# Moving eleven DMA calls of a written-out schedule to later places

## The chip, the cores and the metric

The kernel runs on one core of one Trainium2 chip. The metric is device time in microseconds (us) of one launch. A core has a TensorE (PE, with its weight loads written PEld), a VectorE (DVE), a ScalarE (ACT), a GpSimd (POOL) and a SyncE (SP), and 16 DMA engines that its queues share. All data DMAs of this kernel are issued by SyncE.

## The reference

Two attention blocks, A and B, each on an input x of 2048 tokens by 640 channels, with 32 heads of 20. Their outputs lie side by side in the result.

```python
# A: attention over a sliding window of 256 tokens
qkv = x @ wqkv                                  # 640 x 1920
scores = einsum("bhqd,bhkd->bhqk", q, k) * Dh ** -0.5
mask = (i - j >= 0) & (i - j < 256)
o = einsum("bhqk,bhkd->bhqd", softmax(where(mask, scores, -1e9)), v);  a = o @ wo

# B: linear attention, not causal
phi = lambda t: where(t > 0, t + 1, exp(t)) + 1e-6
kv = einsum("bhsd,bhse->bhde", phi(k), v);  z = phi(k).sum over s
o = (phi(q) @ kv) / (phi(q) @ z + 1e-6);        b = o @ wo
out = concatenate([a, b], axis=-1)
```

## The kernel before

The 2048 tokens are four superblocks of 512 (s = 0 to 3). Block A's attention is cut into 76 score tiles (16 for s = 0, 20 for each other; `tiles_of`, line 39). One tile is a set of small score matmuls into one PSUM tile (L773), one exponential over it on ACT (L793), masks on POOL (L814), and, two tiles later, the products with the values (L841). These tiles follow one another in program order (the loop at line 1103).

Between tiles PE is filled with everything else: the projections q, k and v of A (`a_rows`, `a_v`), B's keys (`b_keys`), the sums of B's keys with its tokens (`b_sums`, L556), B's queries (`b_q`) and the output products. That filler work is a list `plan` of pairs (t, work), where t is in units of tiles. `at(t0, t1, gen, n)` spreads the n banks (PSUM tiles) of one generator evenly over t0 to t1; `do(t0, t1, fns)` does the same with plain calls, which here mostly issue DMAs. `fill_of` (line 1077) sorts all by t and runs through them; after each tile, `take` draws as many columns of matmul work from it as the tile's credit allows. A plain call yields no columns: it is made when the sorted list comes to it. So t sets the order of the work and only roughly its time.

All these DMAs go to SyncE's instruction stream (`nc.sync`) in the order in which the calls are made. SyncE takes them in order; when one has to wait (for its source to be written, or for its buffer to be free), all behind it wait too. The names that matter here:

- `load_part(n, s, tb)` (L958): transposes 128 tokens of x of block n, superblock s, from DRAM into xA or xB, 160 KB. `parts` makes four of them. xA and xB have two buffers each.
- `load_tok(s)` (L548): loads 512 tokens of B's x, not transposed, 640 KB, into `tok` (two buffers); `b_sums(half)` reads them for two superblocks at a time.
- `keep_x(s)` (L947) writes xB of superblock s to DRAM scratch, 640 KB; `again_x(s)` (L951) reads it back for `b_q`.
- `late_load("B", 2)` and `late_load("B", 0)` (L166): B's value and query weights, 800 KB each into wB.
- `moves` (L385, L394): A's q and k rows that need other partitions go through DRAM scratch. The four writes are posted with `soon(write, 3)`: they are made when the third PSUM bank after the last one of q or k is begun. The four reads are calls of the plan (`reads_of`); each first makes all posts that are still open.
- `turn` (L882): transposes A's normalised output within SBUF, also posted with `soon`.

Of the kernel before, what the change touches and what calls it, by code (L numbers as in the profile page):

```python
# [102 lines left out]
def kernel(  # L103
# [228 lines left out]
    for c in range(KT):  # L332
        m = EXTRA * c
        while m < EXTRA * (c + 1):
            n = min(EXTRA * (c + 1) - m, DH - m % DH)
# [209 lines left out]
    def load_tok(s):  # L545
        x_tok[s] = rp.tile([P, TPS, D], BF16, name="tok")
        src = xsrc["B"][s * SB : (s + 1) * SB, :].rearrange("(t p) d -> p t d", p=P)
        nc.sync.dma_start(out=x_tok[s], in_=src)  # L548
# [397 lines left out]
    def keep_x(s):  # L946
        nc.sync.dma_start(out=x_scr[s], in_=xB[s].rearrange("p k n -> p (k n)"))  # L947

    def again_x(s):
        xB[NS + s] = xp.tile([P, KT, SB], BF16, name="xB")  # L950
        nc.sync.dma_start(out=xB[NS + s].rearrange("p k n -> p (k n)"), in_=x_scr[s])  # L951
# [36 lines left out]
    def late_load(n, w):  # L988

        if w in (0, 2):  # L990
            load_w(n, B_wqkv, w, nc.sync)
        elif n == "A":

            wj = w.rearrange("(g j d) n -> g d j n", j=4, d=DH)
            for g in range(NG):
                lo, hi = g * DH, min((g + 1) * DH, P)
                if lo < P:
                    nc.sync.dma_start(out=wo_sb[n][lo:hi, 0:4, :], in_=wj[g, 0 : hi - lo])
            for j in range(4):
                for g in range(NG):  # L1000
                    lo, hi = max(g * DH, P), (g + 1) * DH
                    if hi > P:
                        nc.sync.dma_start(
                            out=wo_sb[n][32 * j + lo - P : 32 * j + hi - P, 4, :],
                            in_=wj[g, lo - g * DH : DH, j],
                        )
        else:
            g = GH * DH
            whole = w[0 : KT * g, :].rearrange("(c p) n -> p c n", p=g)
            nc.sync.dma_start(out=wo_sb[n][0:g, 0:KT, :], in_=whole)  # L1010
            nc.sync.dma_start(out=wo_sb[n][0 : D - KT * g, KT, :], in_=w[KT * g : D, :])
# [9 lines left out]
    def at(t0, t1, gen, n):  # L1021
        for i in range(n):
            plan.append((t0 + (i + 0.5) / n * (t1 - t0), gen, i == n - 1))

    def do(t0, t1, fns):
        fns = list(fns)
        for i, fn in enumerate(fns):
            plan.append((t0 + (i + 0.5) / len(fns) * (t1 - t0), None, fn))

    def parts(t0, t1, n, s):  # L1030
        do(t0, t1, [lambda tb=tb: load_part(n, s, tb) for tb in range(TPS)])
# [19 lines left out]
        at(t0, t1, b_keys(s), KT)  # L1051
    for half, t0, t1 in ((0, 16.4, 21.5), (1, 33.6, 39.2)):
        at(t0, t1, b_sums(half), KT + 2)
    for s, t in ((0, 6), (1, 11), (2, 23), (3, 24)):
        do(t, t, [lambda s=s: load_tok(s)])
    at(40.4, 42, b_kv(), 2)
    do(42.8, 44.8, [lambda c=c: kv_ready(c) for c in range(3)])
# [6 lines left out]
    for n, s, t0, t1 in (("A", 0, 44.5, 48.5), ("A", 1, 49.2, 54.2), ("B", 0, 55.2, 59.4),  # L1064
                         ("B", 1, 60.2, 64), ("A", 2, 64.4, 68.2), ("B", 2, 69, 73),
                         ("B", 3, 73, 76)):
        at(t0, t1, (a_out if n == "A" else b_out)(s), KT)
    for n, s, t0, t1 in (("B", 1, 5, 9), ("A", 2, 6, 12), ("B", 2, 14, 18), ("A", 3, 16, 24),
                         ("B", 3, 17, 22)):
        parts(t0, t1, n, s)  # L1070
    for s, t0, t1 in ((0, 2, 33.5), (1, 12, 38.5), (2, 20, 45.5), (3, 26, 51.2)):
        do(t0, t0, [lambda s=s: keep_x(s)])
        do(t1, t1, [lambda s=s: again_x(s)])
    for t, n, w in ((13, "B", 2), (20, "B", 0), (40.6, "A", A_wo), (42, "B", B_wo)):
        do(t, t, [lambda n=n, w=w: late_load(n, w)])

    def fill_of(events):
# [87 lines left out]
```

## Time and profile before

| what | value |
|---|---|
| median of three runs | 261.54 us (260.58 to 262.65) |
| the profiled execution | 260.71 us, span 259.0 us |
| TensorE (PE) busy | 245.9 us, 95% of the span |
| ACT busy | 199.9 us, 77% |
| DVE busy | 177.5 us, 69% |
| POOL busy | 171.1 us, 66% |
| data moved by DMA | 35.67 MB, 64.7% of the 16 DMA engines |
| mean granted TensorE clock | 1.000 |

Times in the rows of the profile count from the start of the span. A group's row has the line, the engine, the operation, its output and inputs, the count, and the time; a row of the waits has who waited, for whom, the total, the times and the longest. SPq is SyncE's own instruction queue, where a DMA's row is its issue, not its transfer. "issue" as releaser means that the engine waited for nothing that the profile shows. The rows that carry the argument stand in the prediction.

### The profile page before, as it was taken

What the parts mean: (1) busy time and instruction counts of PE and PEld (TensorE: products, weight loads), DVE (VectorE), ACT (ScalarE), POOL (GpSimd) and SP (SyncE); (2) the same over time, 40 slices, a digit from 0 to 9 for tenths busy, and PEclk for the clock granted to TensorE, in tenths of its full rate; (3) what the DMA queues carried; (4) which work ended last, traced back from release to release, by engine and by line L of the source; (5) the groups of instructions that cost most, each with busy time, mean ns of one, the idle gap of its engine ahead of it and who ended that gap; (6) DMA issues with size and microseconds to landing.
All of it is one profiled execution on the core that took longest, in us unless ns stands there. A gap on an engine that the chain in (4) does not pass through costs nothing.

```text
span 259.0 us, 10625 instructions
## 1 busy us (share of the span) xinstructions
PE 245.9 (95%) x4658; PEld 144.0 (56%) x4705; DVE 177.5 (69%) x308; ACT 199.9 (77%) x260; POOL 171.1 (66%) x211
## 2 busy tenths in 40 slices
PE   7899999999999599999999999999999999999995
PEld 7544446556556455545566655555556564565573
DVE  0445797687745156768656598599899879969562
ACT  3466879898876488887676888888979999988642
POOL 7115787778774845759475796949768595977700
PEclk9999999999999999999999999999999999999999
DMA  6995587889669791501454396534767699672735
GB/s 211 291 260 162 108 215 112 192 256 156 79 92 263 74 285 54 168 5 20 105 142 115 54 181 63 137 65 67 189 101 151 137 123 177 112 174 58 237 35 189
DMA packets 65012, 36.35 MB, mean 140 GB/s; under 512 B 48197, under 2 KB 63941, under 8 KB 64965
## 3 DMA queue, kind: packets, MB, share of 16 engines
q1 hardware_dynamic: 64965, 35.67, 64.7%
q8 instruction: 37, 0.61, 1.0%
q14 instruction: 10, 0.08, 0.1%
HBM read 14.42 MB, written 9.83 MB: 94 GB/s over the span
## 4 chain that ended last, share of the span: by engine, by line
PE 90%; DMA 4%; issue 3%; ACT 1%; SPq 1%; DVE 0%
PE dense L287 50%; PE S_ps L773 11%; PE dense L556 9%; PE dense L841 9%; PE dense L422 8%; DMA phi<-in_A_x_dram 2%; DMA xA<-tok 2%; PE dense L663 1%; PE dense L706 1%; PE dense L635 1%; ACT p L793 0%; SPq L968 0%; PE dense L188 0%; DVE wB L274 0%; SPq L182 0%
## 5 line engine op out<-in xcount | busy, mean ns | idle before, releaser
L793 ACT ACTIVATE p<-S_ps 128x2048 bf16<-128x2048 f32 x76 | 142.3, 1872 | 33.8 <-PE S_ps L773 32.7
L814 POOL TENSOR_SCALAR_AFFINE_SELECT p<-p 128x512 bf16<-128x512 bf16 (+1 forms) x152 | 122.7, 830 | 66.1 <-ACT p L793 63.7
L287 PE MATMUL dense<-xA,wqk 128*128 128x512 bf16 x183 | 47.3, 380 | 1.1 <-issue 0.6
L814 POOL TENSOR_SCALAR_AFFINE_SELECT plow<-p 128x1024 bf16<-128x1024 bf16 x32 | 40.0, 1250 | 0.0
L773 PE MATMUL S_ps<-qpad,kpad 20*128 20x64 bf16 (+3 forms) x1664 | 34.7, 211 | 0.4
L773 PEld LDWEIGHTS <-kpad 20*128 20x128 bf16 (+1 forms) x1664 | 20.1, 97 | 26.8 <-issue 25.5
L422 PE MATMUL dense<-wA,xA 128*128 128x320 bf16 x160 | 27.9, 300 | 3.6 <-issue 2.6
L854 DVE STREAM_TRANSPOSE T<-dense 128x512 f32<-128x512 f32 x32 | 22.8, 711 | 11.3 <-PE dense L841 11.3
L287 PEld LDWEIGHTS <-wqk 128*128 128x128 bf16 x200 | 18.5, 98 | 20.6 <-issue 1.3
L301 DVE TENSOR_SCALAR e<-e 128x512 bf16<-128x512 bf16 x40 | 22.1, 553 | 10.8 <-ACT e L297 10.0
L304 DVE SCALAR_TENSOR_TENSOR phi<-dense,e 128x512 bf16<-128x512 f32 x40 | 27.7, 691 | 1.5
L841 PE MATMUL dense<-p,vA 128*32 128x64 bf16 (+2 forms) x1152 | 26.2, 223 | 0.0
L287 PE MATMUL dense<-wB,xB 128*128 128x128 bf16 (+1 forms) x156 | 25.4, 298 | 0.8 <-issue 0.6
L297 ACT ACTIVATE e<-dense 128x512 bf16<-128x512 f32 x40 | 23.4, 594 | 3.0 <-PE dense L287 2.6
L287 PE MATMUL dense<-wo,oT 128*128 128x128 bf16 (+2 forms) x154 | 24.3, 296 | 1.1 <-issue 0.6
L287 PE MATMUL dense<-xB,wB 128*128 128x512 bf16 x90 | 24.2, 380 | 0.6 <-issue 0.3
L556 PE MATMUL dense<-phi,tok 128*128 128x128 bf16 (+1 forms) x154 | 24.3, 297 | 0.5 <-issue 0.3
L287 PE MATMUL dense<-wB,xA 128*128 128x512 bf16 (+1 forms) x156 | 23.4, 298 | 0.8 <-DMA xA<-tok 0.3
L841 PEld LDWEIGHTS <-vA 128*32 128x32 bf16 x1664 | 21.5, 97 | 2.7 <-issue 0.7
L422 PEld LDWEIGHTS <-xA 128*128 128x128 bf16 x160 | 14.4, 97 | 12.5 <-issue 4.8
L871 DVE TENSOR_TENSOR N<-T,recA 128x320 bf16<-128x320 f32 (+1 forms) x28 | 19.2, 685 | 2.9 <-DMA oT<-N 2.0
L272 ACT ACTIVATE osb<-dense 128x512 bf16<-128x512 f32 (+1 forms) x25 | 13.9, 571 | 6.7 <-PE dense L287 6.7
(68 smaller groups left out, 242.7 us busy)
## 6 DMA issues: line engine op xcount, KB each, us to landing
out_dram<-osb SPq DMA_DIRECT2D x7, 640.0 KB
x_scr<-xB SPq DMA_DIRECT2D x4, 640.0 KB
tok<-in_B_x_dram SPq DMA_DIRECT2D x4, 640.0 KB
xB<-x_scr SPq DMA_DIRECT2D x4, 640.0 KB
wB<-in_B_wqkv_dram SPq DMA_DIRECT2D x3, 800.0 KB
q_scr<-qpad SPq DMA_DIRECT2D x16, 60.0 KB
k_scr<-kpad SPq DMA_DIRECT2D x16, 60.0 KB
qpad<-q_scr SPq DMA_DIRECT2D x16, 60.0 KB
```

The lines of the kernel that those rows point to most:

```text
L287: nc.tensor.matmul(dst, lhsT=lhs(kt), rhs=rhs(kt), start=(kt == 0), stop=(kt == KT - 1))
L297: nc.scalar.activation(out=view(e), in_=src, func=ACT.Exp)
L301: nc.vector.tensor_scalar(out=e[:], in0=e[:], scalar1=1e-6, scalar2=1.0 + 1e-6, op0=ALU.add, op1=ALU.min)
L304: nc.vector.scalar_tensor_tensor(out=dst, in0=src, scalar=0.0, in1=view(e), op0=ALU.max, op1=ALU.add)
L422: nc.tensor.matmul(ps[:, 0 : hh * DH], lhsT=xt[:, kt, tb * P : (tb + 1) * P], rhs=w_sb["A"][:, kt, i * hh * DH : (i + 1) * hh * DH], start ...
L556: nc.tensor.matmul(out, lhsT=lhs(x, pk)[:, tb, :], rhs=rhs(pk, tb), start=(i == 0), stop=(i == len(blocks) - 1),)
L773: nc.tensor.matmul(columns(S_ps[0:keys], j, col, n, step), lhsT=kt[32 * j : 32 * j + DH, g, ko : ko + keys], rhs=q_pad[s][32 * j : 32 * j ...
L793: nc.scalar.activation(out=p.rearrange("p a j q -> p j a q"), in_=S_ps.rearrange("p j (a q) -> p j a q", a=2), func=ACT.Exp, scale=scale,)
L814: nc.gpsimd.affine_select(out=dst, in_=src, pattern=[[0, 4], [0, n // HALF], [sgn, HALF]], compare_op=ALU.is_ge, fill=0.0, base=base, chan ...
L841: nc.tensor.matmul(O_ps[32 * j : 32 * (j + 1), q0 : q0 + n], lhsT=v_flat[kb // TPS % 3][:, at + j * HV : at + j * HV + 32], rhs=of(p, j, c ...
L854: nc.vector.transpose(out=T.rearrange("p b e -> p (b e)"), in_=O_ps[:])
L871: nc.vector.tensor_tensor(out=dst[:, :, at : at + b - a], in0=T[:, :, a - lo : b - lo], in1=r[:].to_broadcast([P, SB // 32, b - a]), op=AL ...
```

## The change

Five lines of the plan are edited. `load_tok(2)` and `load_tok(3)` go from t = 23 and 24 to 24.2 and 28.2; B's fourth x (s = 3) from 17 to 22 to 19 to 25; A's fourth x from 16 to 24 to 25.5 to 33.5; `keep_x(2)` and `keep_x(3)` from 20 and 26 to 26.2 and 30.2; B's query weights from 20 to 32.2. No work is added or left out.

```diff
-    for s, t in ((0, 6), (1, 11), (2, 23), (3, 24)):
+    for s, t in ((0, 6), (1, 11), (2, 24.2), (3, 28.2)):
         do(t, t, [lambda s=s: load_tok(s)])
...
-    for n, s, t0, t1 in (("B", 1, 5, 9), ("A", 2, 6, 12), ("B", 2, 14, 18), ("A", 3, 16, 24),
-                         ("B", 3, 17, 22)):
+    for n, s, t0, t1 in (("B", 1, 5, 9), ("A", 2, 6, 12), ("B", 2, 14, 18), ("B", 3, 19, 25),
+                         ("A", 3, 25.5, 33.5)):
         parts(t0, t1, n, s)
-    for s, t0, t1 in ((0, 2, 33.5), (1, 12, 38.5), (2, 20, 45.5), (3, 26, 51.2)):
+    for s, t0, t1 in ((0, 2, 33.5), (1, 12, 38.5), (2, 26.2, 45.5), (3, 30.2, 51.2)):
         do(t0, t0, [lambda s=s: keep_x(s)])
         do(t1, t1, [lambda s=s: again_x(s)])
-    for t, n, w in ((13, "B", 2), (20, "B", 0), (40.6, "A", A_wo), (42, "B", B_wo)):
+    for t, n, w in ((13, "B", 2), (32.2, "B", 0), (40.6, "A", A_wo), (42, "B", B_wo)):
         do(t, t, [lambda n=n, w=w: late_load(n, w)])
```

## The prediction

> **What bounds the kernel now.** I read the page from the top: busy times, then the chain that ended last.
>
> ```profile
> PE 245.9 (95%) x4658; PEld 144.0 (56%) x4705; DVE 177.5 (69%) x308; ACT 199.9 (77%) x260; POOL 171.1 (66%) x211
> ...
> q8 instruction: 37, 0.61, 1.0%
> ...
> PE 90%; DMA 4%; issue 3%; ACT 1%; SPq 1%; DVE 0%
> ```
>
> TensorE is the bound: 95% of the span, 90% of the last chain. An edit that moves only DMAs can win only where PE stands still, and lose only where it makes PE stand. So the next view is PE's own waits from 14 us on, when the start-up is over, and the timeline row that ends the longest.
>
> ```profile
> PE dense L422 <- issue: 2.6, 1, 2.6
> PE dense L287 <- issue: 2.5, 16, 0.2
> PE dense L287 <- DMA xA<-tok: 0.3, 1, 0.3
> ```
>
> ```profile
> 87.52 0.58 PE L422 MATMUL dense<-wA,xA 128*128 128x320 bf16 x3 [2.64 <-issue]
> ```
>
> PE never waits for a late input of superblock 2. Apart from gaps of at most 0.2 us there is one hole, 2.64 us from 84.88 to 87.52, in the middle of one accumulation (L422), with nothing the profile can name as releaser. The page's row q8 suggests what it is: 37 packets with 0.61 MB, 16.5 KB each, and 4658 + 4705 PE instructions over 37 packets are 253 each. So PE's program comes by DMA in blocks of about 254 instructions. I asked the queue view, stretch by stretch, where such packets begin. In order: 85.0 to 85.2, 97.5 to 97.6, 110.1 to 110.2, 114.7 to 114.8, 129.05 to 129.15 us.
>
> ```profile
> q8 instruction: 1, 0.02, 29.1%
> ...
> q8 instruction: 1, 0.02, 60.3%
> ...
> q8 instruction: 1, 0.02, 59.2%
> ...
> q8 instruction: 1, 0.02, 83.2%
> ...
> q8 instruction: 1, 0.02, 70.7%
> ```
>
> (The share is of 16 DMA engines in that stretch: 0.291 x 0.2 x 16 = 0.93 us, and 0.96, 0.95, 1.33, 1.13 for the others.) The packet that begins at 85.1 lands at 86.0, and PE moves on 1.5 us later. I read the hole as PE out of instructions because this block was fetched late.
>
> Why late? These are SyncE's issues before and after, and what the DMA engines did.
>
> ```profile
> 78.09 0.53 SPq L947 DMA_DIRECT2D x_scr<-xB  x1
> 78.67 0.42 SPq L166 DMA_DIRECT2D wB<-in_B_wqkv_dram  x1
> 79.13 1.92 SPq L958 DMA_TRANSPOSE xB<-in_B_x_dram  x1
> 81.09 1.27 SPq L958 DMA_TRANSPOSE xA<-in_A_x_dram  x1
> 82.41 2.26 SPq L958 DMA_TRANSPOSE xB<-in_B_x_dram  x1
> 89.43 0.38 SPq L548 DMA_DIRECT2D tok<-in_B_x_dram  x1
> 89.86 1.25 SPq L958 DMA_TRANSPOSE xA<-in_A_x_dram  x1
> 91.20 0.52 SPq L548 DMA_DIRECT2D tok<-in_B_x_dram  x1
> 91.83 0.44 SPq L947 DMA_DIRECT2D x_scr<-xB  x1
> ```
>
> ```profile
> 79.20:81.50 2.30, 2.30 (x58) 1.49 (x57) 1.90 (x4) 1.36 (x2) 0.95 (x2) 1.00 0.97 266
> 81.50:84.10 2.60, 2.60 (x96) 2.31 (x89) 1.65 (x4) 1.92 (x2) 0.87 (x2) 1.00 1.05 331
> 84.10:88.00 3.90, 1.26 (x46) 0.89 (x46) 0.00 (x0) 2.56 (x4) 3.83 (x5) 1.00 1.18 118
> 90.30:98.20 7.90, 7.69 (x132) 4.21 (x135) 4.07 (x9) 6.93 (x8) 2.91 (x5) 1.00 0.87 267
> 102.80:107.60 4.80, 4.75 (x44) 2.60 (x42) 2.50 (x4) 4.34 (x5) 4.66 (x6) 1.00 0.56 110
> 107.60:110.00 2.40, 2.35 (x79) 1.46 (x79) 2.32 (x5) 2.15 (x3) 1.24 (x2) 1.00 0.67 259
> ```
>
> The last two columns are DMA share and GB/s. The x_scr write runs from 79.2 to about 81.5 (2.3 us, 1.1 us after its issue), wB to 84.1 (2.6, some of it beside transposes), the three 160 KB transposes to 88.0 (1.3 each). The first of these three is done near 85.2, and the instruction packet begins at 85.1, before the two issued after 81.1. That looks like **one line**: a packet waits for everything queued before it. Three more cases agree. The packet at 97.5 comes as the four transfers issued from 89.43 to 92.3 end (98.2); that at 110.1 as the transfer issued at 106.43 ends (110.0); and the packets at 114.7 and 129.1 met a short line or none. By the Trainium skill, "DMA: Bandwidth & Descriptors", section "Queues, rings and completion order", each DMA engine goes round the queue rows packet by packet, by which an instruction packet would wait for one data packet and not for microseconds; the packets at 85.1, 97.5 and 110.1 speak against that. "Runtime: NRT & Kernel Launch", section "Instruction fetch mechanics", has 16 KiB refills "mostly hidden"; the size agrees with row q8, the hiding fails once here.
>
> **The change part by part.** No operation is added or removed. PE, DVE, ACT and POOL keep their order, since these events yield no columns to the filler. Moved are eleven calls, all SyncE DMAs: B's and A's fourth x (four transposes each), `load_tok(2)` and `(3)`, `keep_x(2)` and `(3)`, and B's q weights. SyncE issues in order and runs ahead until an instruction has to wait, so what counts is not the t of a call but which wait it comes to stand behind. These are the waits there are, and the issues after them.
>
> ```profile
> SPq L548 <- PE dense L556: 4.9, 1, 4.9
> ...
> SPq L385 <- DVE kpad L274: 13.9, 1, 13.9
> SPq L385 <- DVE qpad L274: 6.2, 1, 6.2
> ```
>
> ```profile
> 102.02 1.63 SPq L385 DMA_DIRECT2D q_scr<-qpad  x4
> 104.29 2.09 SPq L394 DMA_DIRECT2D qpad<-q_scr  x4
> 106.43 0.35 SPq L951 DMA_DIRECT2D xB<-x_scr  x1
> 120.75 1.62 SPq L385 DMA_DIRECT2D k_scr<-kpad  x4
> ...
> 128.26 0.59 SPq L951 DMA_DIRECT2D xB<-x_scr  x1
> ```
>
> *Step 1, ahead of `load_tok(2)`.* Only three of B's transposes stay there. Without A's and with keep_x(2) and wB gone, SyncE is through by about 77 us and waits for `tok` (its buffer is freed by L556 at 89.4, the 4.9 us of the first row; 2.6 us earlier if the hole goes). The DMA engines are idle at 81 us. The block that began at 85.1 is then fetched without a line. I take it that a block is asked for when PE enters the last one it holds, 254 instructions before it runs dry. The rows above count 96 + 89 from 81.5 to 84.1 and some 80 of the 46 + 46 up to the hole, so that is at about 81.5. To be there by 84.88 the packet must begin by 84.88 - 1.5 - 0.95 = 82.4: 0.9 us in hand. **-2.64 us**.
>
> *Step 2, `tok`(2), B's last transpose, keep_x(2)* go out from 86.8 us: 2.0 + 1.3 + 2.3 us of DMA against 7.9 us before, with an instruction packet near 95. No loss.
>
> *Step 3, behind the q_scr write.* The third bank after q's last is b_keys(2)'s last, t 26.48, just ahead of A's first transpose at 26.5; so the q_scr write, which waits for qpad until 102.02, now has **seven** moved calls behind it, between the q reads and again_x(0): in order A 0, a q read, tok(3), a q read, A 1, two q reads, keep_x(3), A 2, wB, A 3, again_x(0). Nothing in this list waits again; the next wait is the k_scr write at 120.75. So they aren't spread up to t 32.5, they go out in one run. SyncE's time by the rows above: 1.63 + 4 x 1.3 + 4 x 0.4 + 0.45 + 0.55 + 0.45 is 9.9 us, with up to 1 us more for a transpose behind a full line (the 2.26 at 82.41); again_x(0) goes out at 111.9 to 112.9 in before's time. DMA time: q writes and reads 2.7 (0.56 x 4.8), four transposes 5.2, tok 2.0 (640 KB at the 331 GB/s of the second row; the 7.9 us at 90.3 less 1.3 and 2.3 leaves 2.1 each for its two), keep_x 2.3, wB 2.4, again_x 1.9 (1.6 of it in the last row): 16.5 us. It begins 1.1 us after 102.02 and loses 0.2 to gaps, as I estimate: the line is empty at about **119.8**.
>
> *Step 4, which instruction block meets it.* PE passed 632 matmuls and 640 weight loads between 87.5 and 119.8:
>
> ```profile
> 87.50:119.80 32.30, 31.66 (x632) 18.02 (x640) 21.62 (x39) 26.22 (x33) 20.19 (x24) 1.00 0.36 105
> ```
>
> That is 1272, five blocks of 254. So PE runs dry at about 119.7 unless the block that before fetched at 114.75 has landed. Before, that one met no line. After, at 114.75 it finds the rest of wB, A 3 and again_x(0) ahead of it and begins at 119.8. Landing 0.95 and 1.5 to PE: 122.2, a **new hole of 2.4 us**. The bounds: if again_x(0) falls behind the packet (1.9 us less line), 0.5; if the line were not shared, 0; if the DMAs run 1 us slower than summed, 3.4. I take 2.4, as again_x(0)'s descriptors follow 1.1 us after its issue and come by 114.0 at the latest. The block fetched at 110.1 stays harmless: its line ends with A 1 near 110, it is there at 112.5, and PE runs dry a block earlier than 119.7, on average 32.3 / 5 = 6.5 us: 113.2.
>
> *Inputs.* B's fourth x lands by 91 us (b_keys(3) near 104), tok(3) by 109 (b_sums(1) near 120), A's fourth x by 118 (a_rows q at about 132), wB by 117 (b_q(0) near 140). All hidden; only if that cover went would each cost its own 1.3 to 2.4 us.
>
> Sum against the profiled run (260.71 us, span 259.0): -2.64 + 2.4 = **-0.2**, so 260.5. The median of the three is 0.8 above the profiled run; I keep that difference: **261.2 us**.
>
> **The rivals.**
> 1. *The hole goes and none comes* (20%). For it: a line of 5 us ahead of a packet is longer than any seen here (3 to 4). Against it: the three packets that did wait. 261.54 - 2.64 = **258.9**. Under the Trainium skill's packet-by-packet rule, named above, this would be the result if the old hole had come from the crowding at all.
> 2. *again_x(0) comes behind the packet* (13%): new hole 0.5, **259.4**. For it: 2.26 us for one transpose issue. Against: it needs two or three such.
> 3. *Slower: again_x(1) ahead of the block at 129.1* (12%). PE runs through that block in 3.2 us,
>
> ```profile
> 128.35:131.55 3.20, 3.04 (x142) 2.04 (x137) 2.29 (x5) 2.44 (x3) 1.29 (x2) 1.00 0.73 196
> ```
>
> and the packet begins 0.3 us before again_x(1)'s first bytes (128.26 + 1.1). If again_x(1) comes 0.3 us earlier against PE, the packet waits 1.9 us more and the hole is about 2: 261.2 + 2 = **263.2**. The issue hangs on k's evacuation, and that on PE, as before; that speaks against it.
> 4. *The change does not do it* (5%): the block at 85 is late even with no line (0.9 us in hand, of which beginning takes a part), and step 4's hole comes on top: 261.54 + 2.4 = **263.9**.
>
> **How the numbers follow.** Forecast, hole moved: 50%, 260.2 to 262.2 by itself (1 us of DMA time either way). Rivals 20, 13, 12 and 5%. The range leaves out the lower half of rival 1 and the upper tail of 3 and 4: 258.8 to 263.2. One per cent, 2.6 us, is about what a measurement of this kernel can tell from no change. Faster by more than that (under 258.9) is half of rival 1 and, as the three runs of before lie 2 us apart, some 6 points of rival 2 and the forecast: 16%; slower by more (over 264.2), from 3 and 4 with their scatter: 10%; between them 74%.
>
> **What would show it.** Right: PE has no "issue" wait near 85; SyncE issues nothing between about 77 and 86; from 99.4 it issues some eleven microseconds without a break; an "issue" hole of about 2.4 us near 117, with an instruction packet that began as the line ended. Wrong: no such hole, with the packet begun amid the line (rival 1); a hole near 129 (rival 3); one still near 85 (rival 4); a PE wait on a DMA of xB, tok, xA or wB, by which step 3's inputs were too late.

## The result, and the profile after

The changed kernel takes 257.75 us (median of six runs, 257.39 to 259.17), the kernel before 261.87 us (six runs, 260.58 to 262.65): ratio 0.986, 95% interval 0.983 to 0.990. It is 1.4% faster; the forecast was 261.2 us, no change, with a range from 258.8 that the result falls below.

The page of the changed kernel, the rows that answer to the first fence of the prediction (busy times, instruction packets, last chain):

```profile
PE 251.1 (98%) x4705; PEld 144.9 (56%) x4705; DVE 178.3 (69%) x308; ACT 200.0 (78%) x260; POOL 171.4 (67%) x211
...
q8 instruction: 37, 0.61, 1.0%
...
PE 93%; DMA 5%; SPq 0%; ACT 0%; DVE 0%; issue 0%; ACTq 0%
```

"issue" has gone from 3% of the chain to 0. PE has 4705 matmul records here and 4658 before, for the same program: 47 records are missing in the trace of before. The block that the prediction put at 254 instructions is therefore about 256: 128 weight loads, which are all recorded, and their matmuls. PE's waits from 14 us on, columns as before (total, times, longest):

```profile
PE dense L287 <- DMA xA<-tok: 0.8, 1, 0.8
PE dense L287 <- DVE wB L274: 0.3, 1, 0.3
```

There is no hole near 85 and, against step 4, none near 118. The start-up differs from run to run (the first score tile's exponential starts at 18.55 us in one trace and at 19.48 in the other), so I compare by the distance of two such exponentials around the old hole. ScalarE's timeline of the kernel before, two tiles that follow one another:

```profile
84.70 1.88 ACT L793 ACTIVATE p<-S_ps 128x2048 bf16<-128x2048 f32 x1
...
90.33 1.88 ACT L793 ACTIVATE p<-S_ps 128x2048 bf16<-128x2048 f32 x1 [3.67 <-PE S_ps L773]
...
241.20 1.88 ACT L793 ACTIVATE p<-S_ps 128x2048 bf16<-128x2048 f32 x1
```

and of the changed one, the same tiles:

```profile
85.71 1.88 ACT L793 ACTIVATE p<-S_ps 128x2048 bf16<-128x2048 f32 x1
...
88.53 1.88 ACT L793 ACTIVATE p<-S_ps 128x2048 bf16<-128x2048 f32 x1 [0.86 <-PE S_ps L773]
...
239.12 1.88 ACT L793 ACTIVATE p<-S_ps 128x2048 bf16<-128x2048 f32 x1
```

From the first to the second it is 5.63 us before and 2.82 after: **2.81 us less at this one place**. From the second to the last tile it is 150.87 and 150.59: nothing is given back. I call the distance of these two exponentials the *step* below.

SyncE did in the changed kernel what steps 1 to 3 said, in the order that they said. Its issues:

```profile
73.93 3.85 SPq L958 DMA_TRANSPOSE xB<-in_B_x_dram  x3
87.63 0.41 SPq L548 DMA_DIRECT2D tok<-in_B_x_dram  x1
...
100.13 1.61 SPq L385 DMA_DIRECT2D q_scr<-qpad  x4
101.78 1.34 SPq L958 DMA_TRANSPOSE xA<-in_A_x_dram  x1
103.22 0.45 SPq L394 DMA_DIRECT2D qpad<-q_scr  x1
103.76 0.40 SPq L548 DMA_DIRECT2D tok<-in_B_x_dram  x1
104.26 0.38 SPq L394 DMA_DIRECT2D qpad<-q_scr  x1
104.69 1.21 SPq L958 DMA_TRANSPOSE xA<-in_A_x_dram  x1
105.96 0.88 SPq L394 DMA_DIRECT2D qpad<-q_scr  x2
106.88 0.36 SPq L947 DMA_DIRECT2D x_scr<-xB  x1
107.28 1.87 SPq L958 DMA_TRANSPOSE xA<-in_A_x_dram  x1
109.20 0.68 SPq L166 DMA_DIRECT2D wB<-in_B_wqkv_dram  x1
109.92 2.22 SPq L958 DMA_TRANSPOSE xA<-in_A_x_dram  x1
112.24 0.52 SPq L951 DMA_DIRECT2D xB<-x_scr  x1
```

Nothing goes out from 77.8 to 87.6, and from 100.13 on the seven moved calls of step 3 go out without a break, behind the one wait on qpad. The transfers are crowded again, some 20 us later. The crowd is seen by PE's instruction fetch: the packet that meets it begins between 115.4 and 115.5 us (row of the queues in that stretch, with a share of 16 engines, 0.588 x 0.1 x 16 = 0.94 us),

```profile
q8 instruction: 1, 0.02, 58.8%
```

and lands at 116.4. How close that was shows in PE's weight loads (PEld), eight of one score tile at the end of the block. In this order: the kernel before, where the block had long landed; the changed kernel; and the run below with again_x(0) ahead, where PE did stop.

```profile
119.64 0.12 PEld L773 LDWEIGHTS <-kpad 20*128 20x128 bf16 x8 [0.42 <-issue]
```

```profile
117.74 0.24 PEld L773 LDWEIGHTS <-kpad 20*128 20x128 bf16 x8 [0.42 <-issue]
```

```profile
116.44 0.12 PEld L773 LDWEIGHTS <-kpad 20*128 20x128 bf16 x7 [0.42 <-issue]
117.19 0.09 PEld L773 LDWEIGHTS <-kpad 20*128 20x128 bf16 x1 [0.63 <-issue]
```

In the run that stopped, the eighth load is the first of the new block. In the changed kernel that load starts at 117.9, 0.1 us late and 1.5 us after the landing; in the traces with a hole PE moved on 1.4 to 1.5 us after the packet had landed. So this block came just in time, **with nothing to spare**: its weight load is held for 0.1 us, and PE's matmuls show no wait.

### The profile page after: what moved, and what is told of

It is laid out like the page before. It is cut to its first block, busy times and chain, and to the rows that moved or that the text cites. A ratio compares the mean times of both kernels' runs of the same rounds, so it can differ in the third digit from the quotient of the medians.

```text
span 257.4 us, 10670 instructions
## 1 busy us (share of the span) xinstructions
PE 251.1 (98%) x4705; PEld 144.9 (56%) x4705; DVE 178.3 (69%) x308; ACT 200.0 (78%) x260; POOL 171.4 (67%) x211
## 4 chain that ended last, share of the span: by engine, by line
PE 93%; DMA 5%; SPq 0%; ACT 0%; DVE 0%; issue 0%; ACTq 0%
PE dense L287 52%; PE S_ps L773 11%; PE dense L556 10%; PE dense L841 9%; PE dense L422 8%; DMA wA<-in_A_wqkv_dram 3%; DMA xA<-tok 2%; PE dense L663 1%; PE dense L706 1%; PE dense L635 1%; PE dense L188 0%; DVE wB L274 0%; SPq L968 0%; ACT vA L272 0%; SPq L182 0%
## 5 line engine op out<-in xcount | busy, mean ns | idle before, releaser
L287 PE MATMUL dense<-xA,wqk 128*128 128x512 bf16 x200 | 50.0, 380 | 0.0
L841 PE MATMUL dense<-p,vA 128*32 128x64 bf16 (+2 forms) x1152 | 26.2, 222 | 0.0
L287 PE MATMUL dense<-wB,xB 128*128 128x512 bf16 (+1 forms) x160 | 25.9, 300 | 0.0
L287 PE MATMUL dense<-xB,wB 128*128 128x512 bf16 x100 | 25.8, 380 | 0.0
L287 PE MATMUL dense<-wo,oT 128*128 128x512 bf16 (+2 forms) x160 | 25.3, 300 | 0.3 <-DVE wB L274 0.3
L556 PE MATMUL dense<-phi,tok 128*128 128x512 bf16 (+1 forms) x160 | 25.1, 300 | 0.0
L287 PE MATMUL dense<-wB,xA 128*128 128x512 bf16 (+1 forms) x160 | 24.1, 300 | 0.8 <-DMA xA<-tok 0.8
L871 DVE TENSOR_TENSOR N<-T,recA 128x320 bf16<-128x320 f32 (+1 forms) x28 | 18.6, 663 | 1.0
```

Source lines behind the costliest of these rows:

```text
L287: nc.tensor.matmul(dst, lhsT=lhs(kt), rhs=rhs(kt), start=(kt == 0), stop=(kt == KT - 1))
L556: nc.tensor.matmul(out, lhsT=lhs(x, pk)[:, tb, :], rhs=rhs(pk, tb), start=(i == 0), stop=(i == len(blocks) - 1),)
L841: nc.tensor.matmul(O_ps[32 * j : 32 * (j + 1), q0 : q0 + n], lhsT=v_flat[kb // TPS % 3][:, at + j * HV : at + j * HV + 32], rhs=of(p, j, c ...
L871: nc.vector.tensor_tensor(out=dst[:, :, at : at + b - a], in0=T[:, :, a - lo : b - lo], in1=r[:].to_broadcast([P, SB // 32, b - a]), op=AL ...
```

## The experiments

Theory T1: an instruction block waits behind data that SyncE has handed to the DMA engines, PE runs dry, and this is the whole of the difference. Rival T2: the crowd slows PE's inputs or PE itself. Rival T3: the packet is late for a reason of its own, and packets of data don't hold it up.

**B's q weights alone.** The kernel before with one number changed.

```diff
-    for t, n, w in ((13, "B", 2), (20, "B", 0), ...
+    for t, n, w in ((13, "B", 2), (32.2, "B", 0), ...
```

> Of the whole change only B's q weights move (t 20 to 32.2). Theory, one line: an instruction block waits for the data queued before it. Without wB's 2.4 us the line that the block near 85 meets ends near 83 to 84, so the hole of 2.6 to 2.8 us shrinks to 0.3 to 1.2, and the time falls by 1.5 to 2.5 us. Rival, packet by packet: the block is late for a reason of its own, the hole stays near 2.7 and the time is that of the kernel before.

Measured: 258.14 us, ratio 0.990 (0.987 to 0.994). The step is 3.13 us, so 0.3 of the hole is left, and the packet began at 82.4. The hole is as expected, and T3, by which it stays near 2.7, fails; the medians are 3.0 us apart, more than the 1.5 to 2.5 expected. One of the eleven moved calls brings most of the gain.

**The instructions moved, the DMAs left.** The kernel before, with 104 warm-up products of one column in place of 28 of 128 columns. (The added line moves all line numbers behind it by one.)

```diff
             for _ in range(n):
+                m = 1 if n > 28 else P
                 nc.tensor.matmul(
-                    ps[:, 0:P], lhsT=z[:, 0, 0:P], rhs=z[:, 0, 0:P], start=True, stop=True
+                    ps[:, 0:m], lhsT=z[:, 0, 0:P], rhs=z[:, 0, 0:m], start=True, stop=True
...
-    dummies = warm_up((28, 3))
+    dummies = warm_up((104, 3))
```

> The kernel before with its DMAs as they are; TensorE's 28 warm-up products of 128 columns at the start become 104 of one column. That puts 152 more instructions ahead of all work and moves every block boundary 76 weight loads earlier in the code. Theory, blocks of 256 instructions: the block that is asked for in the crowd has its predecessor running dry later, near 87.5, and the hole near 85 shrinks to 0 to 0.6 us with no DMA moved; time down 2 to 2.8 us. Rival, the crowd itself slows PE or its inputs: the hole stays at 85 with 2.6 to 2.8 us.

Measured: 259.44 us, ratio 0.993 (0.990 to 0.997). SyncE issues the same crowd at the same time, and PE runs through the place without a gap. SyncE's and PE's timeline:

```profile
77.62 0.53 SPq L948 DMA_DIRECT2D x_scr<-xB  x1
78.20 0.42 SPq L166 DMA_DIRECT2D wB<-in_B_wqkv_dram  x1
78.67 2.30 SPq L959 DMA_TRANSPOSE xB<-in_B_x_dram  x1
...
85.36 0.54 PE L774 MATMUL S_ps<-qpad,kpad 20*128 20x64 bf16 x40
85.83 0.72 PE L423 MATMUL dense<-wA,xA 128*128 128x320 bf16 x4
```

The step is 2.82 us, to the hundredth that of the changed kernel, **with no DMA moved**. This excludes T2: the crowd does no harm to PE but through the block that is fetched in it. (The medians are 1.7 us apart, less than the 2 to 2.8 expected. The work starts later here, with the first exponential at 19.80 against 18.55. The warm-up itself is not longer, 2.93 us against 3.17; the 18 products behind it take 4.67 us, against 3.30 in the run with B's q weights alone. Why is not shown.)

**More data ahead.** The kernel before with `keep_x(2)` made twice, the second time to a scratch that nothing reads; later three times. The edit is that of three writes; with two there is one spare tile.

```diff
+    spare = [tc.dram_tile([P, KT * SB], BF16, name=f"x_spare{i}") for i in range(2)]
+
     def keep_x(s):
         nc.sync.dma_start(out=x_scr[s], in_=xB[s].rearrange("p k n -> p (k n)"))
+        for t in spare if s == 2 else ():
+            nc.sync.dma_start(out=t, in_=xB[s].rearrange("p k n -> p (k n)"))
```

> The kernel before with keep_x(2) made twice, the second time to a scratch that nobody reads: 640 KB and 2.3 us more in the line ahead of the block near 85. Theory, one line: the hole grows from 2.6-2.8 to 4.4-5.0 us and the time by 1.8 to 2.3. Rival, packet by packet: hole and time as before.

> The kernel before with keep_x(2) made three times, 4.6 us more of large packets ahead of the block near 85. One extra write added only 0.5 us to that block's wait (4.2 in place of 3.75). Theory A, the wait is bounded by what the queue takes in advance, counted in time or bytes: the block waits 4.0 to 4.6 us again, the hole is 3.2 to 3.8 us. Theory B, bounded by a count of packets, of which these writes need few: the block waits 6 to 8 us, hole 5 to 7 us.

Measured with two writes: 263.14 us, ratio 1.007 (1.003 to 1.011), step 7.59. The time is the expected one, but not by the expected way: the hole is only half a microsecond longer than in the trace that I predicted from, not 1.8 to 2.3. PE's timeline of that kernel, and its windows behind the hole, with the granted TensorE clock in the third column from the right:

```profile
87.42 0.70 PE L422 MATMUL dense<-wA,xA 128*128 128x320 bf16 x3 [3.12 <-issue]
```

```profile
87.40:91.00 3.60, 3.58 (x18) 2.02 (x19) 1.19 (x2) 0.00 (x0) 1.71 (x2) 0.55 0.27 57
```

The clock is 0.55 for 3.6 us after the hole; PE loses 0.45 x 3.6 = 1.6 us there, which is about the rest of the 1.96 us by which the step grew. With three writes there are 4.6 us more data ahead than in the kernel before, and the hole is again about the same:

```profile
88.09 0.60 PE L422 MATMUL dense<-wA,xA 128*128 128x320 bf16 x3 [3.34 <-issue]
```

(a single run, 262.56 us, step 7.83). The packet began at 85.7, amid wB's packets, 4.5 us after PE had entered the block before; 3.75 in the kernel before, 4.2 with two writes. So T1 holds, but the line is not without end: **no packet after the start-up of any trace here began more than 4.5 us after PE had entered the block before**, however much stood ahead. (The first packet of the program, at 7 to 18 us, when the inputs are loaded, began up to 5.7 us after by the same count, so that 4.5 us is not a fixed limit.) Theory A of that run is the one that held. What sets the bound is left open: from PE's entry to the packet's begin, on average 101 data packets went to each DMA engine in the kernel before and 38 with three writes, with 67 and 82 KB, so it isn't a count of packets.

**again_x(0) ahead of the block.** The changed kernel with one issue one place earlier.

```diff
-    for s, t0, t1 in ((0, 2, 33.5), ...
+    for s, t0, t1 in ((0, 2, 32.4), ...
```

> The changed kernel with again_x(0) issued one place earlier, ahead of A's last transpose, so that its 640 KB lie ahead of the instruction block asked for near 113. Theory, one line: that block begins near 117.5 in place of 115.4, is 1.2 to 1.9 us late, and a hole of that size opens near 118; time up by as much against the changed kernel. Rival, packet by packet: no hole and the time of the changed kernel.

Measured: 258.67 us (0.987 to 0.994 of the kernel before). PE's timeline has the new hole where step 4 put one, but small:

```profile
117.19 0.28 PE L773 MATMUL S_ps<-qpad,kpad 20*128 20x256 bf16 x1 [0.35 <-issue]
```

The two tiles around it are 3.66 us apart against 3.07 in the changed kernel: 0.6 us, not 1.2 to 1.9. Its packet began at 114.8, 3.9 us after PE had entered the block before. The direction is T1's, the size again that of a bounded line. By the times alone it is not told from the changed kernel.

**again_x(0) later.** The same number the other way, to leave the crowd.

```diff
-    for s, t0, t1 in ((0, 2, 33.5), ...
+    for s, t0, t1 in ((0, 2, 36), ...
```

> The changed kernel with again_x(0) moved from t 33.5 to 36, behind k's scratch reads, so that it leaves the crowd from 102 to 117 us. Theory: in the changed kernel that block lands in time anyway, so no hole goes, and the time is the same within 0.3% (257.4 to 258.4). Rival, the block near 113 is late in some runs of the changed kernel: the scatter above 258.5 goes, and the median falls by 0.3 to 0.5 us.

Measured: 258.77 us, ratio 0.989 (0.981 to 0.997), no version that beats the changed kernel, and above the 257.4 to 258.4 expected. The packet still waits for A's transposes and wB, 2.9 us; there was no hole near 117 to take away. The old hole is not quite gone in this trace: its packet began 1.3 us after PE had entered the block before, and the step is 3.14, 0.3 us longer than in the changed kernel.

**A's fourth x alone, and the scratch writes alone.** One line of the change each, on the kernel before.

> Of the whole change only A's fourth x moves. keep_x(2), wB and B's transposes then go out some 2.5 us earlier, and one transpose less lies ahead of the block near 85. Theory, one line: the line ends near 83.5 to 84, the hole shrinks to 0.8 to 1.8 us. Rival, any part of the change is enough: no hole; rival, only wB counts: hole as before, 2.6 to 2.8.

> Of the whole change only keep_x(2) and keep_x(3) move. 2.3 us of large packets leave the line ahead of the block near 85. B's q weights alone and A's fourth x alone each left a hole of 0 to 0.2 us. Theory, any part that takes over 1.5 us out of what is handed over ahead of that block is enough: hole 0 to 0.8 us. Rival, the writes do not count: 1.8 to 3.1 as in the kernel before.

A single run each: 259.11 us with a step of 2.99, and 259.67 with 3.53. The second is as expected (0.5 us of hole). The first missed its number (no hole where 0.8 to 1.8 was expected): keep_x(2), wB and the transposes went out from 75.3 on, and the line was at its end by 82.4. So each of three parts by itself, B's q weights, A's fourth x or the writes, takes all but 0.2 to 0.7 us of the hole. They don't add up, since the hole is only the part of the packet's wait that exceeds the time in hand.

**The kernel before again, for its trace.** Of the 29 runs of the kernel before that were made beside these kernels (one of 264.62 us, at 0.987, left out), 12 list a mean granted clock of 0.993 or less, with a median of 262.2 us, and 17 one of 0.999 or more, with 260.6. None of the 31 timed runs of the changed kernel and of the four others above without a hole of 1 us or more (q weights, instructions moved, again_x earlier and later) is below 0.999.

> The kernel before once more, for its trace. Half of its runs list a mean granted clock of 0.993 and take about a microsecond longer. Theory, the clock falls behind a hole: the hole near 85 is there in every run, 2.6 to 3.2 us, and where the mean clock is 0.993 the slices right behind the hole show a lower clock, about 0.6 for 4 us, at a cost of 1.2 to 2 us. Rival: the clock falls elsewhere, at random.

> The kernel before, a further trace. The hole was 2.6 us in one trace and 1.8 in another. Theory: where it is 3 us or more the granted clock falls to about 0.6 for the next 4 us and the mean clock is 0.993; where it is under 2.8 us it stays 1.0. Rival: the clock falls without regard to the hole.

> As for the trace before: a hole of 3 us or more goes with a clock of about 0.6 right behind it, a shorter one with 1.0.

Three traces, one wait of PE or timeline row of each, in this order:

```profile
PE dense L422 <- issue: 1.8, 1, 1.8
```

```profile
PE dense L422 <- issue: 1.7, 1, 1.7
```

```profile
86.53 0.98 PE L422 MATMUL dense<-wA,xA 128*128 128x320 bf16 x3 [2.02 <-issue]
```

260.79, 260.76 and 262.06 us. The hole is in every trace, at the same instruction, and from 1.7 to 2.6 us long, so not always the 2.6 to 3.2 expected. It is longest where SyncE is latest (its x_scr write went out at 76.46 to 77.23 in these, at 78.09 in the trace that I predicted from). In the first of these PE also stood 0.9 us at 235.8, with no releaser named, 2.3 us after an instruction packet had landed; stops of 0.6 and 0.8 us at that place are in the traces with two writes and with A's fourth x alone, and what they are stays open. The third has the lower clock, and behind the hole; its window:

```profile
86.50:90.00 3.50, 3.47 (x16) 1.75 (x17) 0.81 (x2) 0.00 (x0) 2.78 (x3) 0.54 0.02 5
```

The rule of 3 us that I had expected falls: the clock fell after 2.0 us of idle PE here and stayed at 1.00 after 2.64 us. That it falls at the hole, and not elsewhere before the kernel's end, the traces with 0.993 show. The same view over 86.28 to 89.69, a little earlier than the window above, has 0.50: half the clock, for 3.41 us. The step of this trace is 6.56, so the hole with the lower clock costs 6.56 - 2.82 = 3.7 us, against 1.9 to 2.0 in the two traces without.

## Why the prediction was wrong

**The bound and the cause (right).** PE was the limit, the hole was PE out of instructions, and the block was late behind the data queued at 78 to 82 us. Moving the boundaries without the DMAs, and the DMAs without the boundaries, both close it.

**Steps 1 and 2 (right).** -2.64 us was forecast, the idle time between modelled ends of matmuls; the step fell by 2.81. Not forecast: the packet at 97.5 us, in the next crowd of transfers, costs 0.1 us in the trace of before, and up to 0.65 in the others, and this goes too.

**Step 3 (right in its order, short in its time).** The order of issues is the one written down, to the place. But from the q_scr write to again_x(0) SyncE took 12.1 us, where I summed 9.9 and at most 1 more: two transposes were held up, 1.87 and 2.22 us in place of 1.3, wB took 0.68. That was rival 2's condition ("two or three such"), which I gave 13%. again_x(0) went out at 112.24, as PE entered the block before, and fell behind the packet.

**Step 4 is the step that failed: the new hole of 2.4 us.** Two terms of it were off. again_x(0) was not ahead of the packet (1.9 us), because of step 3. And the line was taken to be without end: by the sum the packet begins 5.7 us after PE has entered the block before, but even with again_x(0) ahead it began after 3.9 us and the hole is 0.6, and with three writes it began after 4.5. Rival 1 had named this doubt. The moment at which PE runs dry was right: 119.7 on the clock of before is 117.8 on the changed kernel's, which is 1.9 us ahead, and there the weight loads pause. With rival 2's order the line would have ended at 116.0 on that clock and left a hole of 0.5; the packet began at 115.45, and so there was none. That no hole came was luck: the block had nothing in hand.

**Rivals.** Rival 1's outcome came, by rival 2's way. Rival 3 did not come: the block at 127.3 begins 0.8 us after PE enters its last block, as before. Rival 4 did not: in the changed kernel's trace the packet of the old hole begins 0.7 us after PE enters its last block, within the 0.9 us in hand; at 1.3 us, in the run with again_x(0) later, 0.3 us of it came back.

**The sum.** By its own terms step 4's hole is 2.5 us (119.8 + 0.95 + 1.5 - 119.7), and 260.5 + 0.8 is 261.3; neither slip matters. What mattered besides step 4 is that I kept the 0.8 us by which the median of before lay above its profiled run as if it were the kernel's own. A good part of it is the same hole's second cost: behind it the clock can fall, as the three traces with a mean clock of 0.993 have it, and 12 of 29 runs list such a clock; that all 12 fell behind the hole is inferred. The profiled run had the hole at full clock, so its trace could not show that removing the hole is worth 1.9 to 2.8 us in some runs and 3.7 in others; the medians are 4.1 apart, the interval of the ratio spans 2.6 to 4.6.

On the two places where I weighed the Trainium skill. "DMA: Bandwidth & Descriptors", section "Queues, rings and completion order", with its round of the queue rows packet by packet, would have given rival 1's time, which came; yet not its mechanism, as waits of 3.75 to 4.5 us behind data show. The page's packet is typically 9 to 17 descriptors; whether a packet of the profile is one of those no run here shows, so how far the waits contradict the page is open. "Runtime: NRT & Kernel Launch", section "Instruction fetch mechanics", calls the refill "mostly hidden": of 37 refills one came late enough in every trace of the kernel before to stop PE, by 1.7 to 2.6 us, up to 1% of the time, and the one at 97.5 us cost up to 0.65.

## What to carry to other kernels

When an engine with thousands of instructions stops in the middle of an accumulation with no releaser named, look where its instruction packets begin: a block asked for in a DMA crowd can come late, and here it was enough to thin the crowd by one transfer at that moment, or to shift the code against the block boundaries by some instructions. A DMA's place in a written-out order counts only by the wait it stands behind: calls "spread" over seven tiles of the plan went out in 12 us, and here that opened no new hole only because a block came just in time. Price a hole on PE with the clock that may fall behind it, and look at several runs' clocks before one trace is taken for the kernel.

## What the runs showed of the hardware

An instruction packet of 16.5 KB took 0.88 to 1.87 us. It waits behind data already handed over: after the start-up it began up to 4.5 us after PE had entered the block before. At the holes near 85 and 117 PE moved on 1.3 to 1.5 us after the landing. SyncE itself is held up when much is queued: a transpose's issue took 1.2 us alone and up to 2.7 behind a crowd, which may be why more data in the program did not make the wait longer in proportion.

TensorE's granted clock fell to half, for 3.4 us, at holes of 2.0, 3.1 and 3.3 us, and not at holes of 1.7, 1.8 and 2.6 (the windows of 3.5 and 3.6 us that read 0.54 and 0.55 reach a little beyond that stretch). The Trainium skill, "TensorE: Matmul & The Clock Gate", section "Part 1: The HAM clock gate", has half the clock after an idle window of about 3.4 us, with windows that run freely; the 3.4 us at half agree, and free windows would fit that the same length does not always decide, but a fall after 2.0 us of idle is earlier than the page has it.
